# Head triples, a quarter of the exp on VectorE, and one list scheduler for all engines, in a fused attention and FFN kernel

## The chip, the cores and the metric

The kernel runs on one core of a Trainium2 chip. The metric is the device time of one execution, in microseconds (us). ScalarE is called ACT, VectorE DVE, TensorE PE, as in the profile; PEld is TensorE loading weights. The profile gives the clock that was granted to TensorE ("PEclk", as a share of full speed).

## The reference

Input x is 2048 tokens of 640 features. After a layer norm, a multi-query attention (32 heads of 20, one shared key and value head) and a SiLU feed-forward run side by side, and both are added to x.

```python
q = (xn @ wq).reshape(B, S, 32, 20).transpose(0, 2, 1, 3)
k = xn @ wk                      # one key head of 20
v = xn @ wv
scores = einsum("bhqd,bkd->bhqk", q, k) * 20 ** -0.5
o = einsum("bhqk,bkd->bhqd", softmax(scores), v)
out = x + o.transpose(...).reshape(B, S, 640) @ wo + silu(xn @ w1) @ w2    # w1: 640 x 1728
```

The heavy part is elementwise: 32 x 2048 x 2048 exponentials, which is 2048 blocks of 128 keys x 512 queries.

## The kernel before

The queries are cut into four chunks of 512. A step takes up to three heads and one block of 128 keys: three score matmuls with 20 (padded to 32) rows, which run at the same time in three row tiles of the array (in the trace before, at 700.50 us, three start within 0.01 us and take 0.38 us each); one exp over three PSUM banks; three value matmuls in three column tiles (at 700.82 us, in the same way, 0.39 us each), which also give the row sums. Two sets of three banks alternate; bank 6 collects the values, bank 7 serves everything else. In each chunk 32 heads make ten triples and a pair, so there are 704 steps.

```python
def emit_exp(a, t):
    ...
    a.wait_ge(s_S, S_val[t])
    if t >= NE:
        a.wait_ge(s_PV, PV_val[t - NE])
    a.activation(Ebuf[:, t % NE, 0:width], ps[:, base:base + width],
                 AF.Exp, scale=attn_scale).then_inc(s_E, 1)       # the only exp: ScalarE
...
for t in range(T):
    ...
    emit_S(t + NSB, 1)          # scores, two steps ahead
    emit_PV(t)                  # values
    if kt == KT - 1:
        schedule_U_pipeline(t, misc)
    misc_step(BUDGET)           # about one projection matmul per step, until the queue is empty
```

The loop starts when the whole prologue (norm of 16 token tiles, keys, values, first queries) is done.

The softmax here doesn't subtract the row's maximum and nothing guards it: scores larger than these inputs give would overflow.

## Time and profile before

| | before |
|---|---|
| median of the first three executions | 1118.63 us (1108.82 to 1123.88) |
| profiled span | 1109.5 us |
| ACT busy | 90% |
| PE busy | 83%, mean granted clock 0.789 |
| DVE busy | 20% |
| first exp starts | 56.6 us |

The page of the kernel before: busy time per engine, and the busy share in 40 slices of 27.7 us, in tenths. PEclk is the granted clock in tenths.

```profile
PE 917.3 (83%) x5519; PEld 255.4 (23%) x5580; DVE 220.5 (20%) x600; ACT 1000.1 (90%) x819; POOL 24.3 (2%) x61
...
ACT  5599999999989998999989998999998988989994
...
PEclk9899979765579998988559997989557988886556
```

ACT is at 9 nearly everywhere. PE looks busy too, but its clock falls to 5 in four places, one for each query chunk. The groups by shape say what ACT does (line, engine, operation, tiles, shape, count, then busy us and mean ns of one, then idle time before it and who ended it):

```profile
L663 ACT ACTIVATE sbt<-psall 128x1536 bf16<-128x1536 f32 x640 | 882.4, 1494 | 59.8 <-PE psall L590 57.5
L663 ACT ACTIVATE sbt<-psall 128x1024 bf16<-128x1024 f32 x64 | 65.7, 1040 | 10.3 <-PE psall L590 7.6
```

The exp is 948 of 1000 us. Two windows of 20 us from the same trace, one with and one without projection work (columns: window, length, then PE, PEld, DVE, ACT and POOL busy us with counts, granted clock, DMA share, GB/s):

```profile
100.00:120.00 20.00, 15.65 (x105) 4.41 (x105) 7.35 (x16) 19.97 (x19) 0.00 (x0) 1.00 0.00 1
260.00:280.00 20.00, 17.35 (x94) 3.74 (x91) 1.52 (x6) 19.36 (x15) 0.00 (x0) 0.50 0.00 1
```

At half clock PE is *more* busy with less work, and ACT still works 19.4 of 20 us. So where three heads make a step, ACT is the bound.

### The profile page before, as it was taken

What the parts mean: (1) busy time and instruction counts of PE and PEld (TensorE: products, weight loads), DVE (VectorE), ACT (ScalarE), POOL (GpSimd) and SP (SyncE); (2) the same over time, 40 slices, a digit from 0 to 9 for tenths busy, and PEclk for the clock granted to TensorE, in tenths of its full rate; (3) what the DMA queues carried; (4) which work ended last, traced back from release to release, by engine and by line L of the source; (5) the groups of instructions that cost most, each with busy time, mean ns of one, the idle gap of its engine ahead of it and who ended that gap; (6) DMA issues with size and microseconds to landing.
All of it is one profiled execution on the core that took longest, in us unless ns stands there. A gap on an engine that the chain in (4) does not pass through costs nothing.

```text
span 1109.5 us, 13550 instructions
## 1 busy us (share of the span) xinstructions
PE 917.3 (83%) x5519; PEld 255.4 (23%) x5580; DVE 220.5 (20%) x600; ACT 1000.1 (90%) x819; POOL 24.3 (2%) x61
## 2 busy tenths in 40 slices
PE   3778789888888878888898878888898878888888
PEld 2322212221122222222112222222112222222113
DVE  6312321110012332110012232111002331100012
ACT  5599999999989998999989998999998988989994
POOL 8000000000000000000000000000000000000000
PEclk9899979765579998988559997989557988886556
DMA  7200000000000000000000000000000000000000
GB/s 245 96 1 1 1 1 6 13 7 1 1 1 1 1 1 18 12 13 7 1 1 1 1 1 7 18 13 12 1 1 1 1 1 24 1 1 1 1 1 24
DMA packets 9311, 14.86 MB, mean 13 GB/s; under 512 B 1552, under 2 KB 8336, under 8 KB 9248
## 3 DMA queue, kind: packets, MB, share of 16 engines
q1 hardware_dynamic: 7632, 8.69, 2.5%
q0 software_dynamic: 1616, 5.30, 1.4%
q8 instruction: 44, 0.72, 0.3%
q14 instruction: 19, 0.16, 0.0%
HBM read 11.36 MB, written 2.62 MB: 13 GB/s over the span
## 4 chain that ended last, share of the span: by engine, by line
PE 45%; ACT 28%; issue 15%; DVE 9%; POOL 1%; DMA 1%; another core or an unknown queue 1%; DVEq 0%; ACTq 0%; POOLq 0%
ACT sbt L663 25%; PE psall L590 15%; PE psall L622 13%; PE psall L443 4%; PE psall L785 4%; PE psall L738 3%; PE psall L688 3%; PE psall L836 2%; ACT sbt L756 2%; DVE sbt L745 2%; DVE sbt L681 1%; DVE sbt L451 1%; DVE sbt L706 1%; DVE sbt L844 1%
## 5 line engine op out<-in xcount | busy, mean ns | idle before, releaser
L663 ACT ACTIVATE sbt<-psall 128x1536 bf16<-128x1536 f32 (+1 forms) x704 | 947.1, 1453 | 70.0 <-PE psall L590 65.1
L590 PE MATMUL psall<-sbt 32*128 32x512 bf16 x2048 | 339.5, 472 | 67.6 <-ACT sbt L663 46.9
L622 PE MATMUL psall<-sbt 128*32 128x512 bf16 x2048 | 343.2, 477 | 0.4 <-ACT sbt L663 0.2
L590 PEld LDWEIGHTS psall<-sbt 32*128 32x128 bf16 x2048 | 70.7, 94 | 316.2 <-ACT sbt L663 224.2
L622 PEld LDWEIGHTS psall<-sbt 128*32 128x32 bf16 x2048 | 72.2, 96 | 222.3 <-issue 216.8
L738 PE MATMUL psall<-sbt 128*128 128x512 bf16 (+1 forms) x259 | 88.7, 404 | 28.8 <-DVE sbt L745 23.9
L785 PE MATMUL psall<-sbt 128*128 128x128 bf16 (+3 forms) x432 | 100.2, 328 | 10.5 <-DVE sbt L792 5.5
L681 DVE COPY sbt<-psall 96x512 f32<-96x512 f32 (+1 forms) x44 | 30.2, 687 | 319.9 <-PE psall L622 319.9
L688 PE MATMUL psall<-sbt 96*128 96x96 f32 (+1 forms) x176 | 39.8, 318 | 33.1 <-DVE sbt L681 13.4
L745 DVE TENSOR_SCALAR sbt<-psall 128x512 bf16<-128x512 f32 (+1 forms) x56 | 38.6, 690 | 137.3 <-PE psall L738 135.0
L443 PE MATMUL psall<-sbt 128*128 128x512 bf16 x148 | 48.8, 418 | 10.6 <-DVE sbt L451 7.1
L792 DVE TENSOR_TENSOR sbt<-psall,sbt 128x512 f32<-128x512 f32 (+1 forms) x32 | 15.7, 491 | 177.5 <-PE psall L785 177.5
L785 PEld LDWEIGHTS psall<-sbt 128*128 128x128 bf16 x448 | 29.8, 102 | 67.6 <-issue 46.5
L836 PE MATMUL psall<-sbt 128*128 128x128 bf16 (+1 forms) x150 | 33.8, 334 | 7.2 <-DVE sbt L844 3.2
L766 DVE SCALAR_TENSOR_TENSOR sbt<-sbt 128x512 bf16<-128x512 bf16 (+1 forms) x56 | 38.0, 680 | 0.0
L756 ACT ACTIVATE sbt<-sbt 128x512 bf16<-128x512 bf16 (+1 forms) x56 | 37.4, 667 | 0.0
L688 PEld LDWEIGHTS psall<-sbt 96*128 96x128 f32 (+1 forms) x176 | 22.0, 167 | 61.6 <-DVE sbt L681 33.1
L738 PEld LDWEIGHTS psall<-sbt 128*128 128x128 bf16 (+1 forms) x280 | 18.5, 98 | 74.0 <-DVE sbt L745 36.3
L451 DVE CAST sbt<-psall 128x512 bf16<-128x512 f32 x24 | 16.6, 690 | 75.8 <-PE psall L443 73.0
L844 DVE TENSOR_TENSOR sbt<-psall,sbt 128x512 bf16<-128x512 f32 (+1 forms) x32 | 15.3, 490 | 56.6 <-PE psall L836 50.8
L706 DVE TENSOR_TENSOR sbt<-psall,sbt 128x60 bf16<-128x60 f32 (+1 forms) x176 | 26.1, 210 | 1.5
L699 DVE RECIPROCAL sbt<-psall 128x12 f32<-128x12 f32 (+1 forms) x44 | 10.1, 230 | 77.8 <-PE psall L688 77.8
(47 smaller groups left out, 176.8 us busy)
## 6 DMA issues: line engine op xcount, KB each, us to landing
sbt<-in_A_x_dram SPq DMA_DIRECT2D x32, 160.0 KB, 2.5
out_dram<-sbt SPq DMA_DIRECT2D x16, 160.0 KB, 1.8
sbt<-in_B_w_dram POOLq DMA_DIRECT2D x5, 432.0 KB, 5.4
sbt<-in_B_w_dram POOLq DMA_DIRECT2D x13, 160.0 KB, 6.6
sbt<-in_A_wq_dram SPq DMA_DIRECT2D x5, 160.0 KB, 3.7
sbt<-in_A_wo_dram POOLq DMA_DIRECT2D x5, 160.0 KB, 6.9
sbt<-in_A_wv_dram POOLq DMA_DIRECT2D x5, 5.0 KB, 3.2
sbt<-in_A_wk_dram POOLq DMA_DIRECT2D x5, 5.0 KB, 2.3
```

Of the source, the lines that this page charges most:

```text
L443: return pe.matmul(bk(b, 0, QW), wq_pad[:, c, ht * P:(ht + 1) * P], xnT[:, c, qc * QW:(qc + 1) * QW], start=(c == 0), stop=(c == DC - 1))
L590: return pe.matmul(s_out_ap(t, i), kT_rep[s_ * HSLOT:(s_ + 1) * HSLOT, kt * P:(kt + 1) * P], qT[s_ * HSLOT:(s_ + 1) * HSLOT, ht, par, :], ...
L622: return pe.matmul(ps[i * HSLOT:(i + 1) * HSLOT, UB * BANK:UB * BANK + QW], v_aug[:, kt, :], Ebuf[:, e, e_col(i):e_col(i) + QW], start=(kt ...
L663: a.activation(Ebuf[:, t % NE, 0:width], ps[:, base:base + width], AF.Exp, scale=attn_scale).then_inc(s_E, 1)
L681: Ufree_val[n] = EI("dve", lambda v, upar=upar, rows=rows: v.tensor_copy(U_sb[0:rows, upar, :], ps[0:rows, UB * BANK:UB * BANK + QW]), s_U ...
L688: return pe.transpose(ps[:, b * BANK + qt * RS: b * BANK + qt * RS + rows], U_sb[0:rows, upar, qt * P:(qt + 1) * P], ident_f[0:rows, 0:rows])
L738: return pe.matmul(bk(b, 0, HWID, rows=rows), w1_sb[:, c, fk * P:fk * P + rows], xnT[:, c, hb * HWID:(hb + 1) * HWID], start=(c == 0), sto ...
L745: return lambda v: v.tensor_scalar_mul(h_half[0:rows, slot, :], bk(b, 0, HWID, rows=rows), 0.5)
L756: a.activation(t_buf[0:rows, slot, :], h_half[0:rows, slot, :], AF.Tanh).then_inc(s_th, 1)
L766: E_("dve", lambda v: v.scalar_tensor_tensor(out=hT[0:rows, hb % 2, fk, :], in0=t_buf[0:rows, slot, :], scalar=1.0, in1=h_half[0:rows, slo ...
L785: return pe.matmul(bk(b, 0, N_), hT[0:rows, hpar, fk, hcol:hcol + P], w2_sb[0:rows, fk, e0:e1], start=(fk == 0), stop=(fk == FC - 1))
L836: return pe.matmul(bk(b, 0, N_), oT[:, opar, c, i * P:(i + 1) * P], wo_sb[:, c, e0:e1], start=(c == 0), stop=(c == DC - 1))
```

## The change

The intent is to take one head's exp in three from ACT, wherever DVE has time for it (503 of the 2048 blocks, a quarter), and give it to the idle DVE, and to place every instruction by one list scheduler that plans all engines together.

- The heads of all chunks form one row of 128 units, cut into 42 triples and a pair across chunk borders: 688 steps.
- In a step that the scheduler picks (503 of 688), ACT does two heads (1024 columns). DVE does the third: the score already comes scaled so that its integer is the bit pattern of a bf16 power of two. DVE clips it to int16 (z), masks the mantissa into a number y between 1 and 2, multiplies z's bf16 value by y, and masks the power of two out of z. Two value matmuls (of the product and of the power of two) are added later with weights 1 and 2, so that the sum is a quadratic in the mantissa times a power of two.
- DVE does the three operations after the clipping in batches of four such steps (2048 columns).
- Steps start when the first four token tiles are ready, and projection jobs are spread by number over 0.9 of each chunk.

The diff rewrites the file (1015 lines become 1204). Its core, with cuts:

```diff
-def emit_exp(a, t): ...
-    a.activation(Ebuf[:, t % NE, 0:width], ps[:, base:base + width], AF.Exp, scale=attn_scale)
+NZ = 3
+ZB = 4
+PACE = 0.9
+    def want_dve(self, t):
+        if self.pro_left:                 # not before the prologue's last key job
+            return False
+        back = sc.t["dve"] - sc.t["pe"]   # DVE's planned backlog
+        ...
+        return back < DVE_TH
+    def do_S(self, t, now):
+        ...
+        dv = self.want_dve(t)
+        ...                               # three score matmuls
+        na = nh - 1 if dv else nh
+        def efn(a):
+            return a.activation(self.E[:, b0 * QW:(b0 + na) * QW],
+                                self.ps[:, par3 * BANK:(par3 + na) * BANK], AF.Exp, scale=ACT_SCALE)
+        if dv:
+            def p1(v):
+                return v.tensor_scalar(self.Z[:, zs, zp * QW:(zp + 1) * QW], self.bk(bb), 0.0, ZMAX, ALU.max, ALU.min)
+        ...
+        if self.zblocks and (len(self.zblocks) == ZB or t - self.zblocks[0][0] >= ZWAIT or t == self.T - 1):
+            self.flush_z()
+    def flush_z(self):
+        v.tensor_scalar(Y, Z, 0x7F, 0x3F80, ALU.bitwise_and, ALU.bitwise_or)     # y
+        v.tensor_tensor(yb, zb, yb, ALU.mult)                                    # z * y
+        v.tensor_scalar(Z, Z, 0x7F80, None, ALU.bitwise_and)                     # power of two
+    def fill_chunk(self, c, t):
+        ...
+        span = PACE * (s1 - s0)
+        for k, mk in enumerate(jobs):
+            j = mk(s0 + int(span * k / len(jobs)))     # a job's earliest step, by its number
+            self.misc.append(j)
```

## The prediction

> **What bounds the kernel now.** ScalarE. The page's first part gives ACT 1000 us of 1109.5 (90%), PE 83%, DVE 20%. The groups by shape show why: 640 exp of 128x1536 from PSUM keep ACT busy 882.4 us (1.38 us each in sequence, 1.49 alone) and 64 of 128x1024 65.7 us. The first exp starts at 56.6 us, the last ends at about 1094: ACT works some 95% of these 1037 us. Its waits are mostly for the score matmul (65.1 us). PE is second. In stretches without projection work the granted clock is 0.50 and a round of three tiled matmuls takes 0.54 us (timeline); with it the clock is 0.9 to 1.0 and a round takes 0.32 us.
>
> **What the change moves, by the built instruction order.**
> - ACT: 688 steps instead of 704; 499 of 1024 columns, 179 of 1536, 10 of 512. 1024 columns should cost about 0.95 us in sequence (1.38 less 512 columns at 0.85 ns). Sum 474 + 247 + 5, plus 56 tanh at about 0.6: about 760 us against 983.
> - DVE: 503 evictions of 128x512 to int16 (0.69 us alone for this shape, about 0.63 in sequence: 317 us), and 126 times three operations on 2048 columns. [...] No trace shows such an operation yet[...]. Other DVE work is about 160 us. Sum about 770 us against 220.
> - PE: the same 2048 score matmuls, 503 extra value matmuls as a fourth parallel column tile (nearly free), about 195 us of projection streaming at full clock as before. Runs of one tiling mode fall from about 1910 to 1240; a change costs about 0.1 us (0.32 against 0.21 for a round[...]). Sum about 620 us at full clock, 1110 at half.
> - Prologue: steps begin once four of 16 token tiles are ready, about 20 us instead of 57. Tail about 15 us as before.
>
> **Critical path.** Nearly all of ACT's saving is on it, as ACT bounds almost everywhere. But the kernel turns from one bound to two equal ones, ACT 760 and DVE 770, with PE near, in fixed order, and with PSUM only two steps deep. I expect each to be busy about 90% between first and last step: 770/0.9 = 855, plus about 25 us of start and tail.
>
> **Predicted: 880 us**, 8 in 10 between 830 and 950. Chances: faster 0.97, same 0.02, slower 0.01. Projection work spread evenly should hold PE's clock near 1.0 (mean above 0.9 against 0.789).
>
> **What would show each step.** Groups: exp of 1024 near 0.95 to 1.03 us x499; eviction 0.69 x503[...]. Page: ACT and DVE 85 to 90% busy, PE 80 to 88%. First exp at about 20 us. Chain of waits split between ACT, DVE and PE. Waits: ACT for PE's scores, PE for DVE's eviction where the 2048-column product stands in front of it.
>
> **What would make it wrong.** [...] If the clock falls to 0.5 for a third of the time, PE bounds and the time is 930 to 970. If DVE's batches hold PSUM, waits of up to 1 us every fourth step add 50 to 100 us. If the fixed order fits the chip well, 820 to 840.

Passages are cut from the prediction where the trace before had not shown what they say: the durations of a batch's three operations with their term in DVE's sum, a condition on the speed of the bit operations, and a remark each on the norm and on the change of tiling mode. DVE's sum came to about 770 us; 317 us of evictions and 160 us of other work are what stands of it, while 855 and 880 us still rest on the whole sum. "No trace shows such an operation yet" is said of the batch's operations.

What stands can be held against the traces (own readings, from each start to the next). In the trace before, 1024-column exps that another instruction follows directly took 0.954 us (four of them; 0.95 predicted), and DVE evictions of 128x512 from PSUM (L745, 37 of them) 0.607 us (0.63). The 0.85 ns a column lies between (1450 - 1024)/512 = 0.83 (window of 300 to 320 us) and (1494 - 1040)/512 = 0.89 (whole trace). A fourth column tile is nearly free: in the trace after, at full clock, a value round after one of three matmuls started 0.216 us later, and after one of four also 0.216 (medians). Two score rounds in a row were 0.215 us apart there at the least. The 195 us of projection are an estimate; the columns of these matmuls in the trace before come to some 185 us at 0.215 us for 512. What stands under "What would make it wrong" are estimates. A third of 1110 us and two thirds of 855 come to 940, within the 930 to 970; for the waits of up to 1 us no trace was named, and the longest of value matmuls for a batch in the trace after is 1.0 us (L656 on L697).

## The result, and the profile after

The changed kernel takes 907.82 us (904.07 to 909.75, five executions) against 1118.63 us (1108.82 to 1131.95, five). The ratio of fast executions is 0.8115 (95% interval 0.8069 to 0.8162). A ratio here is the mean time of one kernel's fast runs over that of the other's of the same rounds, so it is not quite the ratio of the medians.

| | before | after | predicted |
|---|---|---|---|
| time | 1118.63 us | 907.82 us | 880 (830 to 950) |
| ACT busy in the profile | 1000.1 us | 760.4 us | about 760 |
| DVE busy | 220.5 us | 782.5 us | about 770 |
| PE busy | 83% | 85% | 80 to 88% |
| mean granted clock | 0.789 | 0.888 | above 0.9 |
| first exp starts | 56.6 us | 19.1 us | about 20 us |

The page after, slices of 22.6 us:

```profile
PE 763.0 (85%) x6099; PEld 259.3 (29%) x6099; DVE 782.5 (87%) x1281; ACT 760.4 (84%) x755; POOL 26.5 (3%) x53
...
DVE  7759989988888989899997999999978978878995
ACT  4469999998888799999988888999987868989980
...
PEclk9589989887659999899967999999979898969999
```

There are now two engines at 8 to 9 tenths instead of one. ACT's 4, 4, 6 at the start is the prologue. The clock still dips (6, 5 in slices 11 and 12), and there ACT is at 8; before, it was at 9 in the first such dip (5, 5 in slices 10 and 11). The groups by shape:

```profile
L632 ACT ACTIVATE sbt<-psall 128x1024 bf16<-128x1024 f32 x499 | 491.9, 1039 | 63.3 <-PE psall L616 29.8 <-PE psall L664 19.8 <-PE psall L656 10.9
L632 ACT ACTIVATE sbt<-psall 128x1536 bf16<-128x1536 f32 x179 | 259.9, 1462 | 41.5 <-PE psall L616 22.4 <-PE psall L664 10.3 <-PE psall L656 7.8
L646 DVE TENSOR_SCALAR sbt<-psall 128x512 int16<-128x512 f32 x503 | 340.7, 685 | 75.1 <-PE psall L616 72.4
L696 DVE TENSOR_TENSOR sbt<-sbt 128x2048 bf16<-128x2048 bf16 x125 | 151.7, 1214 | 1.3
L693 DVE TENSOR_SCALAR sbt<-sbt 128x2048 int16<-128x2048 int16 x125 | 86.1, 689 | 2.9
L697 DVE TENSOR_SCALAR sbt<-sbt 128x2048 int16<-128x2048 int16 x125 | 85.0, 680 | 0.2
```

The two bit operations on int16 take 689 and 680 ns for 2048 columns and the product 1214.

Windows of the trace after:

```profile
80.00:100.00 20.00, 18.35 (x150) 5.84 (x148) 19.26 (x30) 18.71 (x19) 0.00 (x0) 1.00 0.00 1
240.00:260.00 20.00, 17.23 (x109) 3.91 (x106) 16.32 (x25) 16.64 (x17) 0.00 (x0) 0.52 0.00 1
300.00:320.00 20.00, 19.03 (x160) 8.00 (x157) 16.46 (x27) 14.16 (x15) 0.00 (x0) 1.00 0.11 34
```

The first is the good state: full clock, DVE 19.3 and ACT 18.7 of 20 us. In the second, at half clock, both fall to about 16.5, while PE is no busier by count (109 matmuls instead of 150): each takes longer. The third is a planned PE-bound stretch, with the output projection of the chunk before and a full clock. PE's rounds at both clocks, from the timeline (start, length, instruction; one round of parallel tiles is several lines with the same start):

```profile
302.28 0.39 PE L656 MATMUL psall<-sbt 128*32 128x512 bf16 x2
302.50 0.38 PE L656 MATMUL psall<-sbt 128*32 128x512 bf16 x2
...
249.48 0.64 PE L656 MATMUL psall<-sbt 128*32 128x512 bf16 x3
249.91 0.64 PE L656 MATMUL psall<-sbt 128*32 128x512 bf16 x2
```

At full clock the next value round starts 0.22 us later, at half clock 0.43 us. A change of tiling mode costs more: at full clock a value round starts 0.32 us after the score round before it (301.96 to 302.28 us here, 700.50 to 700.82 in the trace before). The mode change accounts for the 0.1 us between 0.22 and 0.32.

### Where the time went, step by step

The kernel builds its instruction order from planned durations, so it holds a plan: a start time for each of its 688 exps, and a planned total of 840.8 us. The trace gives the real starts. Subtracting one from the other, in stretches of eight exps sorted by the clock granted in them, gives this (own reading of the trace of 902.2 us; "lag" is time lost against the plan):

```
                                  stretches  us on chip  lag gained
before the first exp                                       4.9
first 16 exps (prologue)              2         41.8       3.9
full clock (mean above 0.97)         51        477.2       2.1
part of the time at half clock       25        259.8      31.0
half clock (mean up to 0.6)           7         75.9      17.4
```

At full clock the plan holds almost exactly over 477 us. Of the 59 us of lag at the last exp, some 48 arise where the clock was not full; the other 11 are mostly the start and the prologue. This is a correlation so far, and the experiments below were made to test it.

ACT was busy about 753 of the 862 us between its first exp (19.1 us) and its last (880.8 us). Of the 109 us idle, some 20 lie in the prologue (window of 20 to 60 us: busy 20.5 of 40), about 48 are the lag in dipped stretches, and the rest, about 40, is in the plan, most of it where the output projection makes PE the bound (14.16 of 20 us above).

### The profile page after: what moved, and what is told of

It reads as the page before. It is cut to its first block, busy times and chain, and to the rows that moved or that the text cites. A ratio compares the mean times of both kernels' runs of the same rounds, so it can differ in the third digit from the quotient of the medians.

```text
span 902.2 us, 15485 instructions
## 1 busy us (share of the span) xinstructions
PE 763.0 (85%) x6099; PEld 259.3 (29%) x6099; DVE 782.5 (87%) x1281; ACT 760.4 (84%) x755; POOL 26.5 (3%) x53
## 5 line engine op out<-in xcount | busy, mean ns | idle before, releaser
L632 ACT ACTIVATE sbt<-psall 128x1024 bf16<-128x1024 f32 (+2 forms) x688 | 730.6, 1143 | 104.8 <-PE psall L616 52.3
L646 DVE TENSOR_SCALAR sbt<-psall 128x512 int16<-128x512 f32 x503 | 340.7, 685 | 75.1 <-PE psall L616 72.4
L616 PE MATMUL psall<-sbt 32*128 32x512 bf16 x2048 | 293.2, 422 | 77.0 <-ACT sbt L632 57.6
L656 PE MATMUL psall<-sbt 128*32 128x512 bf16 x1545 | 226.1, 428 | 23.5 <-DVE sbt L697 12.1
L662 PE MATMUL psall<-sbt 128*32 128x512 bf16 x503 | 181.0, 426 | 0.0
L664 PE MATMUL psall<-sbt 128*32 128x512 bf16 x503 | 173.6, 428 | 0.0
L696 DVE TENSOR_TENSOR sbt<-sbt 128x2048 bf16<-128x2048 bf16 x126 | 152.7, 1212 | 1.3
L656 PEld LDWEIGHTS psall<-sbt 128*32 128x32 bf16 x1545 | 55.0, 99 | 127.4 <-issue 54.1
L693 DVE TENSOR_SCALAR sbt<-sbt 128x2048 int16<-128x2048 int16 x126 | 86.7, 688 | 2.9
L828 PE MATMUL psall<-sbt 128*128 128x320 bf16 x448 | 85.1, 307 | 0.8 <-DVE sbt L841 0.4
L697 DVE TENSOR_SCALAR sbt<-sbt 128x2048 int16<-128x2048 int16 x126 | 85.5, 679 | 0.2
L662 PEld LDWEIGHTS psall<-sbt 128*32 128x32 bf16 x503 | 41.5, 98 | 0.0
L794 DVE SCALAR_TENSOR_TENSOR sbt<-sbt,psall 128x512 bf16<-128x512 bf16 (+1 forms) x56 | 38.0, 678 | 2.5 <-ACT sbt L789 2.4
L718 PE MATMUL psall<-sbt 128*128 128x64 f32 x172 | 35.9, 311 | 4.5 <-DVE sbt L794 2.3
L664 PEld LDWEIGHTS psall<-sbt 128*32 128x32 bf16 x503 | 37.4, 97 | 0.0
```

What stands on the lines that cost most here:

```text
L616: ins = pe.matmul(self.bk(par3 + j), self.kT[r:r + SLOT, kk, kt * P:(kt + 1) * P], self.qT[r:r + SLOT, h // 4, (x // H) % 2, :], start=Tru ...
L632: return a.activation(self.E[:, b0 * QW:(b0 + na) * QW], self.ps[:, par3 * BANK:(par3 + na) * BANK], AF.Exp, scale=ACT_SCALE)
L646: return v.tensor_scalar(self.Z[:, zs, zp * QW:(zp + 1) * QW], self.bk(bb), 0.0, ZMAX, ALU.max, ALU.min)
L656: ins = pe.matmul(self.bk(UBANK, 0, QW, q * SLOT, (q + 1) * SLOT), self.v[:, kt, :], self.E[:, (b0 + j) * QW:(b0 + j + 1) * QW], start=fir ...
L662: pe.matmul(self.bk(UBANK, 0, QW, 64, 96), self.v[:, kt, :], y, start=first, stop=last, tile_position=(0, 64))
L664: ins = pe.matmul(self.bk(UBANK, 0, QW, 96, 128), self.v[:, kt, :], z, start=(gd == 0), stop=(self.last_dve_kt[g] == kt), tile_position=(0 ...
```

## The experiments

Two theories. The **clock theory**: the time above the plan is lost because TensorE's granted clock falls to half, and here, unlike before, nothing has slack to hide it. The **rival**: the loss is DVE's (long batches, misjudged durations), and the clock is only a companion. Experiments of one session ran on one chip, beside the kernel before; sessions are compared by ratio. All results were correct.

### e3: the scheduler without exp on DVE

```diff
     def want_dve(self, t):
-        if self.pro_left:
-            return False
+        return False
```

> One part alone: the new scheduler, prologue and head triples, but no step's exp on VectorE; all on ScalarE. The plan is 1012.7 us. If the parts add up as in the prediction: 1020 to 1045 us, ScalarE busy about 980 us, so of the 211 us gained some 80 to 95 are the scheduler's and the prologue's and 115 to 130 the exp moved to VectorE. Clock theory says that the clock may fall here as in the kernel before (mean below 0.85) and that it costs little, since ScalarE bounds. Rival: a new scheduler brings nothing by itself, 1090 to 1110.

Measured: 1044.29 us, ratio 0.9399 (0.9335 to 0.9462), ACT busy 966.4 us, mean clock 0.803. In the session the kernel before took 1113.25 us. So scheduler, triples and prologue bring about 69 us of the gain (80 to 95 were expected). The changed kernel's ratio of 0.8115 would be about 903 us here, so moving the exp brings the other 140 or so (115 to 130 expected). The rival's 1090 to 1110 is out. A window of this run:

```profile
260.00:280.00 20.00, 17.73 (x94) 4.02 (x91) 1.33 (x3) 19.77 (x16) 0.00 (x0) 0.50 0.00 1
```

At half clock ACT works 19.77 of 20 us. With ACT as the only bound the clock costs little: read against its own plan as above, this run lost 22 us in the 677 us at less than full clock, where the changed kernel lost 48 in 336.

### e1, e2, e4: three tries at the clock through the projection work

My first form of the clock theory was that the clock falls where a chunk's projection work has run out. e1 makes that stretch longer, e2 puts unused matmuls into it, e4 paces the jobs by their matmul time so that it vanishes.

```diff
 e1
-PACE = 0.9
+PACE = 0.6
 e2
+        if c < QC - 1:
+            for st in range(s0 + int(span), self.first_step[c + 1] + 18, 3):
+                self.misc.append(self.dummy_job(st))      # two 128x512 matmuls into bank 7, no reader
 e4
-PACE = 0.9
+PACE = 0.95
-        s0 = self.first_step[c]
-        s1 = self.first_step[c + 1]
-        ...
-            j = mk(s0 + int(span * k / len(jobs)))
+        s0 = self.first_step[c] + 20
+        s1 = self.first_step[c + 1] + (20 if c < QC - 1 else 0)
+        ...
+            j.min_step = max(j.min_step, s0 + int(span * done / sum(cost)))   # done: matmul time so far
```

> One constant: projection jobs are spread over 0.6 of each query chunk instead of 0.9, so the stretch without projection work at the end of a chunk grows from a tenth to four tenths. The kernel's own list scheduler plans 840.9 us for it, as for the changed kernel (840.8), with 499 steps on VectorE against 503. Clock theory (the changed kernel loses some 50 us against its plan because TensorE's granted clock falls to 0.5 where projection work is missing): slower, about 920 to 940 us, mean clock below 0.86. Rival (the loss against the plan comes from VectorE's long batches and misjudged durations, wherever it is shown): the same within 1%, 900 to 915.

> Useless work added: in the stretch at the end of each of the first three chunks, and the first 18 steps of the next, two 128x512 matmuls into the projection bank every third step, read by nobody. The plan is 841.4 us against 840.8, with 505 steps on VectorE. Clock theory: faster although TensorE does more, 875 to 895 us, clock 1.0 in those stretches and mean above 0.92. Rival (VectorE batches and durations): the same or some us slower, 905 to 915.

> Projection jobs are paced by their matmul time instead of by their number, over 0.95 of a chunk, shifted by 20 steps so that they last until the next chunk's first jobs can start. The plan is 840.9 us, as for the changed kernel, with fewer stretches of low planned TensorE load (11 of 6 us instead of 18). Clock theory: faster, 880 to 898 us, mean clock above 0.91. Rival: the same, 902 to 912.

Measured: e1 914.34 us (ratio 0.8215, clock 0.877), e2 911.52 us (0.8194, 0.89), e4 914.83 us (0.823, 0.877). Their intervals (0.815 to 0.8277 together) overlap that of the changed kernel's control, run as e5 below (0.8103 to 0.8265). The clock theory in this form missed: e1 should have taken 920 to 940 us, and e4 and e2 should have gained 10 to 30 us. The dips had only moved. But in all three traces the lag was again found outside the full-clock stretches: in e2, for one, 447 us at full clock gained 1.3 us of lag, 372 us of the others 56.6.

So the trigger was wrong. The clock records of the traces change in multiples of 3.41 us. I counted, for each such window, the columns that PE streamed, a 32-row score tile or a 32-column value tile counting as a quarter of a full-array matmul, and looked at the next window's clock. Over twelve traces (all but e6):

```
columns streamed in a      full clock now:            half clock now:
window of 3.41 us          windows, of them next half  windows, of them next half
   0 to 1500                   22     22                   46     46
1500 to 2400                  141    138                  275    256
2400 to 2800                  110     69                  129     94
2800 to 3200                  141     42                  151     57
3200 to 4000                  458      6                  150     15
4000 and more                1533      0                    -      -
```

At full clock a window has room for about 8000 columns, an estimate from 512 in 0.22 us. After one window under about 2800, a third, the next one is mostly at half clock (229 of 273); the limit is not sharp (42 of 141 between 2800 and 3200). No long gap without work goes before it here. Between 60 and 880 us of the changed kernel's trace the longest PE idle gap is 1.6 us, and in the half-clock stretch from 220 to 272 us 0.9 us. A step with exp on DVE streams 384 + 512 columns, and a step takes about 1.17 us (477.2 us for 408 exps at full clock), which makes some 2600 in a window: the attention alone sits just under the limit. And the value matmuls of four steps wait for one DVE batch and then come together, so that windows without any may stand between windows with many; that this bunching matters is not shown, for batches of two (e11 below) left the clock as low. The plan of the changed kernel has 31.5 of 225 windows under 2816 columns (mean over six positions of the window grid), e1's 36.0, e2's 26.8, e4's 35.5; the traces have 174, 199, 170 and 198 us at half clock after the first 60 us. The order is the same, but the control e5, which is the changed kernel once more, has 190, so such differences are partly chance.

### e5, e6, e7: the control, and score rounds issued twice

To raise the streamed columns with little else changed (the scheduler plans anew: 506 steps with exp on DVE in e6, 508 in e7, against 503), a score round is issued twice into the same banks; the second writes the same values over the first.

```diff
+        rep = self.repeats(now, nh)     # 2 where the plan streamed too little in the last 2 us, else 1
-            for j, x in enumerate(us):
+            for j, x in list(enumerate(us)) * rep:
```

> The changed kernel itself, unaltered, as a control on the same chip as the next three. Expected 903 to 914 us, mean clock 0.88 to 0.89, and some 51 clock windows of 3.4 us at half clock after the first 50 us, as in its first trace.

> The clock theory, sharpened by the first runs: a window of 3.41 us in which TensorE streams under about 2800 full-array columns (a 32-row score tile or a 32-column value tile counted as a quarter) is followed by a window at half clock; in the changed kernel's plan 31.5 of 225 windows are that low. Here 205 of the 688 score rounds are issued twice into the same banks (same result), where the plan has streamed under 2400 columns in the last 2 us. Plan 844.8 us against 840.8, low windows 12.5 against 31.5, TensorE 52 us more work. Clock theory: faster than the control by 20 to 35 us, mean clock above 0.94. Rival (the loss against the plan is VectorE's or the semaphores'): slower than the control by 4 us or more.

> Every score round after the prologue issued twice: 674 rounds more, TensorE 160 us more work; the plan grows to 895.6 us, with 3 low windows. Clock theory: about the control's time in spite of it, 900 to 920 us, the loss against the plan down from 61 us to some 15, mean clock above 0.97. Rival: the plan's 55 us come on top, 950 to 965 us.

Measured: control 910.93 us (ratio 0.8184, clock 0.878), e6 903.97 us (0.8093, clocks 0.875 to 0.929 in four executions), e7 932.91 us (0.8361, clock 0.965). e6 went the right way, though its 7 us fall well short of the 20 to 35 that the theory promised and the intervals overlap; its profiled execution also had 0.949 instead of 1.0 as the upper clock, so its trace is no clean comparison. e7 is the clearer one: 674 useless rounds lengthen the plan by 54.8 us, and the kernel gets only 22 us slower. The excess of the profiled span over the plan fell from 67.9 us (control: 908.7 against 840.8) to 38.1 us (933.7 against 895.6). The rival's 950 to 965 us did not come, nor did the clock theory's 920: about 30 us of the loss went away with the dips. e7's page:

```profile
PE 857.4 (92%) x8110; PEld 266.3 (29%) x8110; DVE 794.5 (85%) x1289; ACT 762.7 (82%) x755; POOL 26.4 (3%) x53
...
PEclk9569999999999999899999999999999999899999
```

### e8 and e11: DVE batches of two steps

```diff
-NZ = 3
-ZB = 4
+NZ = 6
+ZB = 2
```

> VectorE's batches hold two steps instead of four, in six buffers instead of three of the same total size; 252 batches of three operations on 1024 columns. VectorE has some 26 us more work for the fixed costs, yet the plan is 827.3 us against 840.8, with 25 low windows against 31.5. If the plan is right in this: 875 to 895 us. If VectorE bounds, as the prediction's sum had it (770 us against ScalarE's 760): slower than the control, 915 to 935 us.

> Batches of two alone, once more, as the control of these two: 875 to 891 us at mean clocks of 0.87 to 0.90, as in its first four executions.

Measured: e8 887.45 us in the session of the control (910.93), ratio 0.7892 against 0.8184; of its four executions two were slow (890.79 and 890.7 us at clock 0.873, against 875.35 at 0.898 and 884.2 at 0.884), the profiled one among them; the ratio is of the other two. e11, the same kernel with more rounds: 888.83 us, ratio 0.7937 (0.7898 to 0.7975). So batches of four cost some 20 to 27 us (e11's ratio against the changed kernel's 0.8115 and against the control's 0.8184). The groups by shape of e11:

```profile
L696 DVE TENSOR_TENSOR sbt<-sbt 128x1024 bf16<-128x1024 bf16 x253 | 170.9, 682 | 1.2
L697 DVE TENSOR_SCALAR sbt<-sbt 128x1024 int16<-128x1024 int16 x253 | 103.4, 414 | 0.2
L693 DVE TENSOR_SCALAR sbt<-sbt 128x1024 int16<-128x1024 int16 x253 | 100.9, 418 | 0.4
```

DVE's work grows, from 782.5 to 800.0 us on the pages, and the kernel is faster. So DVE's amount of work was not the limit. (The busy times of the three groups, 375 us against 325, count time twice where one operation starts before the last has ended. Counted from each start to the next, the three take 332 us against 303: own reading of the traces; e8's expectation named 26 us more. The fixed costs show in the masks: 680 to 689 ns for 2048 columns, 414 to 418 for 1024.) The plan says why in part (827.3 us against 840.8). For the rest the waits say what changed, not what caused it. The changed kernel's trace first, then e11's: PE's value matmuls waiting for the last operation of a batch (us in total, times, longest):

```profile
PE psall L656 <- DVE sbt L697: 12.1, 26, 1.0
```

```profile
PE psall L656 <- DVE sbt L697: 10.0, 24, 0.9
```

DVE's eviction waiting for the scores:

```profile
DVE sbt L646 <- PE psall L616: 72.4, 120, 1.9
```

```profile
DVE sbt L646 <- PE psall L616: 40.0, 66, 1.5
```

And the weight loads of the next scores waiting for DVE's eviction, which frees their PSUM bank (us in total, times):

```profile
  PEld psall L616: 61.2, 100
```

```profile
  PEld psall L616: 31.7, 54
```

The wait for the batch itself hardly fell; the two waits around the eviction fell by nearly half. This points to evictions that stand behind a long batch and hold their bank, but no run isolates it. The clock did not gain: 198 (e8) and 177 us (e11) at half clock after 60 us, as before.

### e9, e10: both

e9 is e8 with e6's doubling (199 rounds), e10 the same with a higher limit, so that it doubles 356 rounds.

> Both edits that helped: VectorE's batches of two steps, and a score round issued twice where the plan has streamed under 2400 columns in 2 us (199 rounds). Plan 828.9 us, low windows 4.5 (batches of two alone: 827.3 and 25). Clock theory, scaled to what the first use of the doubling brought (7 us of 20 to 35 expected): 865 to 880 us, 5 to 20 us faster than batches of two alone, mean clock above 0.92. Rival (doubling's gain was chance or belonged to the batches of four): equal to batches of two alone within 4 us, or slower.

> The same with the doubling wherever under 3200 columns were streamed in 2 us (356 rounds). Plan 837.0 us, low windows 2.2. Clock theory: mean clock above 0.95, 865 to 885 us; if the plan's 8 us extra weigh more than the windows saved, slower than with 2400.

Measured in one session, six executions each:

| | plan | low windows planned | half clock after 60 us | mean clock of the executions | median | ratio |
|---|---|---|---|---|---|---|
| e11, no doubling | 827.3 | 25.3 | 177 us | 0.864 to 0.886 | 888.83 | 0.7937 |
| e9, 199 doubled | 828.9 | 4.5 | 52 us | 0.948 to 0.962 | 860.06 | 0.7677 (0.7639 to 0.7715) |
| e10, 356 doubled | 837.0 | 2.2 | 10 us | 0.974 to 0.978 | 857.50 | 0.7662 (0.7631 to 0.7692) |

The pages of e11 and of e10:

```profile
PE 757.6 (86%) x6057; PEld 257.3 (29%) x6103; DVE 800.0 (91%) x1669; ACT 755.4 (86%) x755; POOL 26.6 (3%) x53
...
PEclk9569999898559999888966999989975999999999
```

```profile
PE 768.8 (90%) x7107; PEld 256.1 (30%) x7163; DVE 805.7 (94%) x1684; ACT 750.9 (88%) x755; POOL 26.4 (3%) x53
...
PEclk9589999999989999999999999999999999999999
```

And the same stretch of both traces, e11 first:

```profile
240.00:260.00 20.00, 16.84 (x115) 4.33 (x116) 17.34 (x37) 16.98 (x18) 0.00 (x0) 0.59 0.00 1
```

```profile
240.00:260.00 20.00, 18.50 (x209) 5.53 (x205) 19.10 (x41) 19.50 (x19) 0.00 (x0) 0.97 0.00 1
```

Useless matmuls on a PE that was already 86% busy make the kernel 31 us faster: 209 matmuls instead of 115 recorded in the stretch, and DVE and ACT both fuller. e10 lags its plan by 17 us at the last exp, of which 9 are there by the 16th exp, in the prologue. Both kernels came out a little faster than the clock theory said (865 us at best). As the reason for the time above the plan, the rival is out; that long batches cost something by themselves is shown by e8 and e11. e10 has the lowest median, with e9 not clearly behind it (their intervals overlap): 857.5 us against 907.82 for the change as made, a ratio of 0.7662 against 0.8115.

## Why the prediction was right or wrong

The time, 907.82 us, lies in the range of 830 to 950, and 28 us above the 880 named.

- **ACT bounds before**: right (ACT was busy 968 of the 1038 us from first to last exp, 93%, where the prediction has some 95%). e3 shows it again, with ACT at 19.77 of 20 us at half clock.
- **ACT falls to about 760 us**: right (760.4), and in its parts. The instructions of one engine overlap at their ends (the product of 1.23 us at 304.73 us is followed at 305.87), so a group's busy time is more than its share of the engine's. Counted from each start to the next (own reading of the trace), 1024 columns took 0.956 us against 0.95 predicted, and 1536 took 1.353 against 1.38.
- **DVE rises to about 770 us**: right (782.5), in the sum and nearly in the two terms. Counted in the same way an eviction cost 0.628 us (0.63 predicted), and the other work was 164 us (160). A batch cost 2.41 us, or 303 us in all.
- **"Each to be busy about 90%"**: between first and last exp ACT was busy 753 of 862 us, 87%, and DVE 759, 88%. The 862 us against 855 predicted is 7 of the 28 us. The 90% was worked out from nothing in the trace, and what it stood for was in good part another loss: of ACT's 109 us idle, some 48 came with the clock, which the prediction held near full. That the figure came so close is partly luck.
- **"Plus about 25 us of start and tail"**: too small. 19.1 us before the first exp and 21.4 after the last are 40.5, so 15 us of the miss. The prediction named 20 and 15 itself and then added only 25. The remaining 6 us are executions longer than the profiled 902.2 us.
- **Steps begin at 20 us instead of 57**: the first exp does start at 19.1 us, but until 58 us only 14 of the 688 are issued, and ACT is busy 20.5 of the 40 us from 20 to 60. About half of that head start was kept.
- **The clock, "mean above 0.9"**: wrong, 0.888 in the profile, 0.87 to 0.89 in the executions. This is the step whose mechanism failed. "Projection work spread evenly" was thought to hold the clock; e4 spread it more evenly and gained nothing. The trace before already spoke against it: from 210 to 220 us and from 230 to 240 us 16 and 14 projection matmuls (L785, the second feed-forward product) ran, and the clock was 0.50. The clock was at half for some 22% of the span. What the counts point to instead is whether each single window of 3.41 us streams about a third of what it could; raising the low windows by doubled rounds is worth 31 us (e11 to e10).
- **"If DVE's batches hold PSUM ... 50 to 100 us"**: batches did cost, but some 20 to 27 us (e8, e11). That they hold PSUM is likely but not isolated: with batches of two, the waits of score weight loads for DVE's eviction fell from 61.2 to 31.7 us.
- **The chain of waits** could not be checked: the chain on the page after ends at the last instruction and shows 0% for every line.

Open: about 40 us of ACT idle time that is in the plan, most of it where the output projection bounds PE. No run changed that. And why e6, with batches of four, gained only 7 us where e9 gained 29 with as many doubled rounds; e6's plan keeps 12.5 low windows against 4.5, and its trace 119 us at half clock after 60 us (control 190) against e9's 52 (e11 177), which fits, but e6's trace had the other upper clock.

## What to carry to other kernels

When work moves from one bound engine to another so that two or three are near their limit, read the granted clock window by window and not as a mean: a dip that costs little under one bound (22 us in 677 in e3) costs more when nothing has slack (48 in 336). Where the clock falls after windows in which TensorE streams little, filling them with useless rounds where the engine has time can pay, as it did here (31 us). And do not size a batch by its fixed costs alone: shorter batches gave DVE some 28 us more work in the three operations and made this kernel 20 to 27 us faster.
